# FFT layer and top-2 expert layer on one core: mixed last units, earlier re-reads, one addition on another engine

## The chip, the cores and the metric

One core of a Trainium2 chip runs the whole program. The metric is device time in microseconds (us): the median of three runs, lower is better. TensorE (PE) multiplies matrices, VectorE (DVE) and ScalarE (ACT) work on elements, GpSimd (POOL) works on elements and issues the indirect DMAs, SyncE (SP) issues the other DMAs.

## The reference

```python
X = np.fft.rfft(x, axis=1)                       # x: (8, 2496, 256)
y = np.fft.irfft(X * (filt_r + 1j * filt_i), n=2496, axis=1).astype(np.float32)
x = y.reshape(19968, 256)
logits = x @ w_gate + np.log1p(np.exp(x @ w_noise)) * noise      # 8 experts
top2 = the two largest logits of each row, softmaxed over the two
for e in range(8):
    for k in range(2):
        mask = top2[:, k] == e
        out[mask] += top2_w[mask, k, None] * (np.maximum(x[mask] @ w1[e], 0) @ w2[e])   # 256 -> 1024 -> 256
```

## The kernel before, in words

**The FFT side** takes the batches in turn, each as two halves `n` of 128 columns. A transform of 2496 points is a two-stage product, 39 by 64, written as matmuls. Between the forward and the inverse transform stands the filter: `kg1` (line 404) takes a product `p` from PSUM, multiplies it by `fr` and `fi`, and adds or subtracts the two results (lines 428 and 433). `kg2` (line 436) reads that result as weights of the matmuls of line 446. `kg1` and `kg2` run five times (`kg` 0 to 4) for each half `n`. For `n` under 4, the first two batches, the addition or subtraction is on GpSimd; afterwards it is on VectorE.

**The gate and the routing** turn the logits into lists of rows for each expert. The rows of `y` lie in DRAM. An expert unit gathers its rows from there with an indirect DMA of GpSimd (line 1156) into slots of one ring buffer (`slot("xg")`, four slots of 128 rows), and has them transposed by a DMA (line 1195).

**The expert side** runs in units of rows of one expert. `expert` (line 1332) does eight hidden blocks for a unit (PSUM tile `hps`, ScalarE's `hh` at line 1369, VectorE's `hl` at line 1370), then for each 128 rows 24 matmuls into `yps`, ScalarE's scaled copy (line 1396) and GpSimd's indirect scatter with addition to `out` (line 1397). All matmuls go as three of 16-bit halves (`_mm3`, lines 123 to 126). Scatters of one unit are declared independent of each other; a scatter of another unit waits until the last unit's have landed, since they may meet in a row of `out`.

**Sizes of units.** Early units have 512 rows, then come units of 1024, seven of 512, and at last the tail: units of 256 and 128 rows (`ENDS`, line 52). With these inputs 14 units of 256 and 4 of 128 are used. The other places for tail units, up to 17 and 8, are in a conditional part that isn't taken (line 1474). Each tail unit loads its own expert's weights from a scaled copy in DRAM (line 1270), into three places in turn.

**Scaling.** From the fifth batch on (`HALF`), rows and weights are scaled by powers of two and split into float16 halves. That wants the largest magnitude of each weight matrix (64 loads, line 595, with ScalarE's squares, line 599) and of the rows so far. Of the first two batches the rows' maxima are not taken when they are made: `load_y` (line 608) reads `y` back in 12 DMAs of 256-byte runs, and `top_y` (line 613) reduces each on VectorE into `ymax`. `powers` (line 553) turns a maximum into a power of two by a PE transpose, some ten small VectorE instructions and two small matmuls. It runs twice for the weights (`wmax`, into `wtab`) and once for each of the last four batches (`xscale`, line 579).

**What sets the order.** The preparation `wscales` (line 588) is a generator of steps. One step is taken for each four writes of the FFT side; the first gather of a unit of the fifth batch takes all that are left (line 1143). The program is written as one interleaved stream of FFT and expert work. The scheduler then orders each engine's queue by a simulated time, with priorities pinned for the first batches. Each engine runs its own queue strictly in order, SP's and POOL's DMA issues included.

Of the kernel before, what the change touches and what calls it, by code (L numbers as in the profile page):

```python
# [22 lines left out]
NB, S, D = 8, 2496, 256  # L23
# [26 lines left out]
NUNIT = (LEFT + E * (UNIT // 2 - 1)) // UNIT  # L50
USUAL = LEFT // UNIT
ENDS = (UNIT, USUAL, NUNIT), (UNIT // 2, E // 2, E)
SW = 32
YW = D + E
LR = 128
# [95 lines left out]
class Moe:  # L151
# [249 lines left out]
    def kg1(self, n, kg):  # L401
        nc, P, h = self.nc, self.P, n % 2
        th, tl = self.tt.pop((n, kg))
        Mh, Ml = self.cM
        p = self.ps("q3")
        if tl is None:
            nc.tensor.matmul(p, self.rM, th, start=True, stop=True)
        else:
            nc.tensor.matmul(p, Mh, th, start=True, stop=False)
            nc.tensor.matmul(p, Mh, tl, start=False, stop=False)  # L410
            nc.tensor.matmul(p, Ml, th, start=False, stop=True)
        if self.early:
            ab = P.tile([128, 2, 4, 128], F32, name="ab", tag="w2", bufs=4)
            a, b = ab[:, 0], ab[:, 1]
        else:
            a = P.tile([128, 4, 128], F32, name="a", bufs=2)
            b = P.tile([128, 4, 128], F32, name="b", bufs=1)
        p3 = p.rearrange("p (k d) -> p k d", k=4)
        fr = self.fr[:, h, 4 * kg:4 * kg + 4]
        fi = self.fi[:, h, 4 * kg:4 * kg + 4]  # L420
        if n >= 2:


            nc.scalar.copy(b[0:64], p3[64:128])
            nc.scalar.copy(b[64:128], p3[0:64])
            nc.vector.tensor_mul(a, p3, fr)
            nc.vector.tensor_mul(b, b, fi)
            (nc.gpsimd if n < 4 else nc.vector).tensor_sub(a, a, b)
        else:
            nc.vector.tensor_mul(a, p3, fr)  # L430
            nc.vector.tensor_mul(b[0:64], p3[64:128], fi[64:128])
            nc.vector.tensor_mul(b[64:128], p3[0:64], fi[0:64])
            (nc.gpsimd if n < 4 else nc.vector).tensor_add(a, a, b)
        self.zz[n, kg] = a

    def kg2(self, n, kg):
# [142 lines left out]
    def xscale(self, bt):  # L579

        nc = self.nc
        nc.vector.tensor_reduce(self.xm, self.ymax[:, :2 * bt + 2], axis=AX.XY, op=ALU.max)
        q = yield from self.powers(self.xm, 1, TX)
        t = self.xs[bt + 1] = self.cp.tile([128, 2], F32, name=f"xs{bt}")
        nc.vector.tensor_copy(t, q[:, :, 0])
        yield

    def wscales(self):


        nc, io, v = self.nc, self.io, self.nc.vector
# [39 lines left out]
        def pairs(first, then, n):  # L631
            old = []
            for i in range(n + 3):
                if i >= 3:
                    self.pin(then, *old.pop(0), hold=False)
                if i < n:
                    old.append((i, self.pin(first, i, hold=False)))
                yield

        yield from pairs(load, top, 8 * E)  # L640
        for a, t in enumerate((TW1, TW2)):
            q = yield from self.powers(self.wmax[:, a * E:a * E + E], E, t, True)
# [3 lines left out]
            else:  # L646
                v.tensor_mul(self.wtab[:, 2], self.wtab[:, 2], q[:, 1])
            yield
        yield from pairs(load_y, top_y, len(Y))
        self.scaled = True  # L650
        yield
        self.pin(load_all, 0)
# [483 lines left out]
    def gather(self, blk, i):  # L1136
# [12 lines left out]
        if self.tail(tabi):  # L1149
            w = self.wodd = (self.wodd + 1) % 3  # L1150
            if nt < BLK // 128:
                w = self.load_planes(tabi, s, w)
        xg = []
        for t in range(nt):
            x = self.slot("xg")
# [250 lines left out]
    def run(self):  # L1406
# [15 lines left out]
        def parts():  # L1422
# [20 lines left out]
            for s in range(SINGLE):  # L1443
                yield from cut(self.read_list(NB, s, BLK), NB)
            self.more = [self.nc.values_load(self.tabs[NB + 1 + i][0:1, 0, n:n + 1], min_val=0, max_val=E * CAPB * BLK // u)  # L1445
                         for i, (u, n, _) in enumerate(ENDS)]
            it = (self.read_list(NB + 1 + i, s, u) for i, (u, n, _) in enumerate(ENDS) for s in range(n))
            soon = [next(it)]
            while soon:
                soon += [b for b in (next(it, None),) if b]  # L1450
# [70 lines left out]
```

## Time and profile before

| | us |
|---|---|
| median of three runs | 2186.98 |
| the runs | 2180.4, 2186.98, 2194.4 |
| the profiled execution | 2191.23 |
| its span | 2189.4 |
| TensorE busy in the span | 2107.5 (96%) |
| VectorE, ScalarE, GpSimd busy | 1473.3, 1286.4, 1024.6 |

The span runs from the first to the last instruction of the profiled execution; 1.83 us of its time lie around the span. Busy times are sums over one engine. TensorE's idle time is what is left of the span when its busy time is taken off; a wait on another engine costs time only where TensorE, or the end of the program, waits for it.

### The profile page before, as it was taken

The page shows a single profiled execution, that of the slowest core. Times are in us where ns is not written, and L with a number is a line of the kernel's source. Part 1 is how long each engine was busy: PE and PEld are TensorE (multiplying, and loading weights), DVE is VectorE, ACT ScalarE, POOL GpSimd, SP SyncE. Part 2 cuts the span into 40 slices and gives each one's busy share as a digit, 9 for nine tenths or more (in the row PEclk, how much of TensorE's full clock was granted, in tenths as well). Part 3 has the DMA queues.
Part 4 walks back from the last instruction along what each step waited for, and adds up shares of the span by engine and source line. Part 5 has one row for each costly group of instructions (what it writes and reads, how often), then busy time and mean ns, then how long its engine had stood idle before and what let it go on. Part 6 is the DMA issues. An engine that isn't in the chain of part 4 may idle for free. (4 is left out here: it accounts for less than half of the span.)

```text
span 2189.4 us, 42880 instructions
## 1 busy us (share of the span) xinstructions
PE 2107.5 (96%) x14517; PEld 1596.5 (73%) x14517; DVE 1473.3 (67%) x3245; ACT 1286.4 (59%) x2505; POOL 1024.6 (47%) x946
## 2 busy tenths in 40 slices
PE   8779999999999999899999999999999999999996
PEld 6437888888888888666666666766666666667886
DVE  4866678767986787778766886579666664333443
ACT  6666774777567746665665556555566564333443
POOL 4133424533443343545544453544566555654653
PEclk9989999999999999999999999999999999999999
DMA  9688987999888866967766666856899999768996
GB/s 241 173 247 203 230 222 171 222 234 228 203 213 230 189 144 152 202 160 174 156 155 151 136 146 149 198 118 131 198 246 238 230 238 211 200 148 221 277 273 170
DMA packets 511675, 428.49 MB, mean 196 GB/s; under 512 B 215680, under 2 KB 397016, under 8 KB 511448
## 3 DMA queue, kind: packets, MB, share of 16 engines
q1 hardware_dynamic: 450135, 341.27, 59.2%
q0 software_dynamic: 61312, 84.40, 22.5%
q8 instruction: 116, 1.90, 0.4%
q14 instruction: 112, 0.91, 0.1%
HBM read 263.92 MB, written 122.03 MB: 176 GB/s over the span
## 5 line engine op out<-in xcount | busy, mean ns | idle before, releaser
L1397 POOL DMA_INDIRECT out<-stage,ids x316 | 527.3, 1669 | 339.8 <-ACT stage L1396 245.9
L1370 DVE SCALAR_TENSOR_TENSOR hl<-hps,hh 128x512 f16<-128x512 f32 (+3 forms) x712 | 432.2, 624 | 339.5 <-ACT hh L1369 279.1
L1156 POOL DMA_INDIRECT stage<-y,ids x316 | 348.4, 1103 | 538.2 <-DMA xt<-stage 425.5
L124 PE MATMUL yps<-w,hh 128*128 128x256 f16 (+1 forms) x2048 | 558.8, 279 | 9.0 <-ACT hh L1369 3.8
L125 PE MATMUL yps<-w,hh 128*128 128x256 f16 (+1 forms) x2048 | 553.2, 277 | 0.0
L126 PE MATMUL yps<-w,hl 128*128 128x256 f16 (+1 forms) x2048 | 543.4, 278 | 6.8 <-DVE hl L1370 6.5
L1369 ACT ACTIVATE hh<-hps 128x512 f16<-128x512 f32 (+3 forms) x712 | 375.6, 550 | 185.7 <-PE hps L126 161.6
L125 PE MATMUL hps<-mxl,w1h 128*128 128x512 f16 (+1 forms) x1024 | 394.3, 386 | 0.7 <-DVE mxl L1244 0.7
L126 PE MATMUL hps<-mxh,w1l 128*128 128x512 f16 (+1 forms) x1024 | 393.0, 385 | 0.0
L124 PE MATMUL hps<-mxh,w1h 128*128 128x512 f16 (+1 forms) x1024 | 385.5, 388 | 2.7 <-DVE hl L1370 1.7
L1396 ACT ACTIVATE stage<-yps,gt 128x256 f32<-128x256 f32 x316 | 143.2, 475 | 342.3 <-PE yps L126 169.8
L124 PEld LDWEIGHTS <-hh 128*128 128x128 f16 x1760 | 172.3, 98 | 51.3 <-ACT hh L1369 4.1
L126 PEld LDWEIGHTS <-hl 128*128 128x128 f16 x1760 | 171.5, 98 | 48.9 <-issue 3.0
L125 PEld LDWEIGHTS <-hh 128*128 128x128 f16 x1760 | 172.2, 98 | 38.1 <-issue 6.0
L126 PEld LDWEIGHTS yps<-w,hl 128*128 128x128 f32 x768 | 145.9, 192 | 15.8 <-DVE hl L1370 8.2
L124 PEld LDWEIGHTS yps<-w,hh 128*128 128x128 f32 x768 | 147.0, 192 | 12.5 <-ACT hh L1369 4.9
L125 PEld LDWEIGHTS yps<-w,hh 128*128 128x128 f32 x768 | 146.6, 192 | 4.4 <-issue 0.6
L542 ACT COPY yt<-q 117x1024 uint16<-117x1024 uint16 x96 | 90.8, 946 | 42.4 <-PE q L536 23.6
L126 PEld LDWEIGHTS <-w1l 128*128 128x128 f16 x640 | 62.6, 98 | 71.8 <-issue 1.1
L1226 DVE COPY stage<-xt 128x1024 uint16<-128x1024 uint16 (+2 forms) x174 | 109.8, 685 | 3.0 <-issue 1.9
L125 PEld LDWEIGHTS <-w1h 128*128 128x128 f16 x640 | 62.6, 98 | 54.0 <-issue 4.0
L124 PEld LDWEIGHTS <-w1h 128*128 128x128 f16 x640 | 62.6, 98 | 53.0 <-issue 6.2
(287 smaller groups left out, 4041.7 us busy)
## 6 DMA issues: line engine op xcount, KB each, us to landing
stage<-w SPq DMA_DIRECT2D x328, 256.0 KB
x<-x SPq DMA_DIRECT2D x88, 256.0 KB
fd<-c SPq DMA_DIRECT2D x77, 240.0 KB
fi<-wpl SPq DMA_DIRECT2D x18, 1024.0 KB
fx<-fd SPq DMA_DIRECT2D x140, 128.0 KB
out<-z SPq DMA_DIRECT2D x24, 702.0 KB
wp<-w SPq DMA_DIRECT2D x64, 256.0 KB
fr<-w SPq DMA_DIRECT2D x16, 1024.0 KB
```

The source lines that it names most:

```text
L124: nc.tensor.matmul(o, lh, rh, start=start, stop=False)
L125: nc.tensor.matmul(o, lh, rl, start=False, stop=False)
L126: nc.tensor.matmul(o, ll, rh, start=False, stop=stop)
L542: e = nc.scalar.copy(yt.bitcast(U16)[:, :k, :256].rearrange("p g (two d) -> p g two d", two=2), p.bitcast(U16)[:RP, :2 * m].rearrange("p ( ...
L1156: self.pin(lambda: nc.gpsimd.indirect_dma_start(out=x.bitcast(I32), out_offset=None, in_=self.y[:BLK + ready * ROWS], in_offset=bass.Indir ...
L1226: nc.vector.tensor_copy(xu.rearrange("p (t two) -> p two t", two=2), ent[3][0][:, 2 * kc:2 * kc + 2, :w])
L1369: hold(lambda: nc.scalar.activation(h, p, AF.Relu))
L1370: v = hold(lambda: nc.vector.scalar_tensor_tensor(l, p, 0.0, hf[0], op0=ALU.max, op1=ALU.subtract))
L1396: nc.scalar.activation(o, p, AF.Copy, scale=gate[:, t])
L1397: a = nc.gpsimd.indirect_dma_start(out=self.io["out"][:BLK + ready * ROWS], out_offset=bass.IndirectOffsetOnAxis(ap=ids[:, t:t + 1], axis= ...
```

## The change

Three parts. The tail units are taken from one list, `MIXED`, in which a unit of 256 rows with number s has key s and one of 128 rows has key 3s + 4, so that the 128-row units stand after the fifth, eighth, eleventh and fourteenth unit of 256; before they stood after all of them. A gather of 256 rows then skips a slot of the ring where a 128-row unit has left it at an odd place. The re-reads of `y` come ahead of the weights' maxima and the two weight chains in `wscales`. In batch 0 the addition of line 433 moves from GpSimd to VectorE; batch 1 stays on GpSimd. (Line numbers of the changed program are 1 higher from line 53 on, and 3 to 5 higher from line 582 on.)

```diff
--- before.py
+++ after.py
@@ -50,6 +50,7 @@
 NUNIT = (LEFT + E * (UNIT // 2 - 1)) // UNIT
 USUAL = LEFT // UNIT
 ENDS = (UNIT, USUAL, NUNIT), (UNIT // 2, E // 2, E)
+MIXED = sorted(((i, s) for i, (_, n, _) in enumerate(ENDS) for s in range(n)), key=lambda u: u[1] * 3 + 4 if u[0] else u[1])
 SW = 32
 YW = D + E
 LR = 128
@@ -425,12 +426,12 @@
             nc.scalar.copy(b[64:128], p3[0:64])
             nc.vector.tensor_mul(a, p3, fr)
             nc.vector.tensor_mul(b, b, fi)
-            (nc.gpsimd if n < 4 else nc.vector).tensor_sub(a, a, b)
+            (nc.gpsimd if 2 <= n < 4 else nc.vector).tensor_sub(a, a, b)
         else:
             nc.vector.tensor_mul(a, p3, fr)
             nc.vector.tensor_mul(b[0:64], p3[64:128], fi[64:128])
             nc.vector.tensor_mul(b[64:128], p3[0:64], fi[0:64])
-            (nc.gpsimd if n < 4 else nc.vector).tensor_add(a, a, b)
+            (nc.gpsimd if 2 <= n < 4 else nc.vector).tensor_add(a, a, b)
         self.zz[n, kg] = a
 
     def kg2(self, n, kg):
@@ -579,6 +580,7 @@
     def xscale(self, bt):
 
         nc = self.nc
+        assert self.seen
         nc.vector.tensor_reduce(self.xm, self.ymax[:, :2 * bt + 2], axis=AX.XY, op=ALU.max)
         q = yield from self.powers(self.xm, 1, TX)
         t = self.xs[bt + 1] = self.cp.tile([128, 2], F32, name=f"xs{bt}")
@@ -637,6 +639,8 @@
                     old.append((i, self.pin(first, i, hold=False)))
                 yield
 
+        yield from pairs(load_y, top_y, len(Y))
+        self.seen = True
         yield from pairs(load, top, 8 * E)
         for a, t in enumerate((TW1, TW2)):
             q = yield from self.powers(self.wmax[:, a * E:a * E + E], E, t, True)
@@ -646,7 +650,6 @@
             else:
                 v.tensor_mul(self.wtab[:, 2], self.wtab[:, 2], q[:, 1])
             yield
-        yield from pairs(load_y, top_y, len(Y))
         self.scaled = True
         yield
         self.pin(load_all, 0)
@@ -1150,6 +1153,8 @@
             w = self.wodd = (self.wodd + 1) % 3
             if nt < BLK // 128:
                 w = self.load_planes(tabi, s, w)
+        while (self.turns.get("xg", -1) + 1) % nt:
+            self.slot("xg")
         xg = []
         for t in range(nt):
             x = self.slot("xg")
@@ -1444,7 +1449,7 @@
                 yield from cut(self.read_list(NB, s, BLK), NB)
             self.more = [self.nc.values_load(self.tabs[NB + 1 + i][0:1, 0, n:n + 1], min_val=0, max_val=E * CAPB * BLK // u)
                          for i, (u, n, _) in enumerate(ENDS)]
-            it = (self.read_list(NB + 1 + i, s, u) for i, (u, n, _) in enumerate(ENDS) for s in range(n))
+            it = (self.read_list(NB + 1 + i, s, ENDS[i][0]) for i, s in MIXED)
             soon = [next(it)]
             while soon:
                 soon += [b for b in (next(it, None),) if b]
```

GpSimd's queue at the end of the used tail units, before. `out` is the scatter of line 1397, its `ids` name the unit, `x2` marks the two halves of a unit of 256 rows, and line 1156 is a gather.

```order
L1156 DMA stage_84<-y_60,ids_28778 128x264
L1397 DMA out<-stage_84,ids_28002 21104x256 x2
...
L1397 DMA out<-stage_84,ids_28198 21104x256
...
L1397 DMA out<-stage_84,ids_28392 21104x256
L1397 DMA out<-stage_84,ids_28584 21104x256
L1397 DMA out<-stage_84,ids_28778 21104x256
```

And now:

```order
L1161 DMA stage_84<-y_60,ids_28698 128x264
L1402 DMA out<-stage_84,ids_27946 21104x256
...
L1402 DMA out<-stage_84,ids_28142 21104x256 x2
...
L1402 DMA out<-stage_84,ids_28334 21104x256 x2
L1402 DMA out<-stage_84,ids_28528 21104x256 x2
L1402 DMA out<-stage_84,ids_28698 21104x256
```

The last four units were four single scatters; they are now three pairs and one single scatter.

VectorE's queue in batch 0, around the filter products of two steps, before (`q3` is PSUM, `fr` and `fi` the filter):

```order
L430 TENSOR_TENSOR ab_245<-q3_243,fr_80 128x512
L431 TENSOR_TENSOR ab_245<-q3_243,fi_81 64x512
L432 TENSOR_TENSOR ab_245<-q3_243,fi_81 64x512
L430 TENSOR_TENSOR ab_285<-q3_283,fr_80 128x512
L431 TENSOR_TENSOR ab_285<-q3_283,fi_81 64x512
```

And now:

```order
L431 TENSOR_TENSOR ab_245<-q3_243,fr_80 128x512
L432 TENSOR_TENSOR ab_245<-q3_243,fi_81 64x512
L433 TENSOR_TENSOR ab_245<-q3_243,fi_81 64x512
L434 TENSOR_TENSOR ab_245<-ab_245 128x512
L431 TENSOR_TENSOR ab_285<-q3_283,fr_80 128x512
```

Each step has a fourth instruction on VectorE ahead of the next step's first.

VectorE's queue at the first expert unit of the fifth batch, before (`xm<-ymax` begins the chain of the rows' scale, `pm`, `pe` and `pq` belong to it, `hl` is the expert block's low half):

```order
L582 TENSOR_REDUCE xm<-ymax 128x1
L615 TENSOR_REDUCE ymax<-wp 117x1 x2
L1202 SCALAR_TENSOR_TENSOR w1l<-stage,sc,w1h 128x512
L1370 SCALAR_TENSOR_TENSOR hl<-hps,hh 128x512
L398 TENSOR_TENSOR tl<-fx,th 128x512
L615 TENSOR_REDUCE ymax<-wp 117x1
```

And now, from the end of that chain (`xs`) on; the rows of `wtab` end a weight chain:

```order
L647 COPY wtab<-xm 128x8
L649 COPY wtab<-xm 128x8
L562 TENSOR_REDUCE pm<-xm 8x1
L563 TENSOR_SCALAR pm<-pm 8x1
L564 TENSOR_SCALAR pe<-pm 8x1
L566 TENSOR_SCALAR pe<-pe 8x1
L567 TENSOR_SCALAR pe<-pe 8x1
L568 TENSOR_SCALAR pq<-pe 8x1
L569 TENSOR_SCALAR pq<-pe 8x1
L570 TENSOR_SCALAR pq<-pq 8x2
L573 TENSOR_SCALAR pd<-ident,pq 8x8 x2
L647 COPY wtab<-xm 128x8
```

The re-reads have left this place, and both weight chains stand in it, the second with nothing between its instructions.

## Rows read from the trace of the kernel before

**Rows 1.** The page, part 1: busy us, share of the span and instructions of each engine.

```profile
PE 2107.5 (96%) x14517; PEld 1596.5 (73%) x14517; DVE 1473.3 (67%) x3245; ACT 1286.4 (59%) x2505; POOL 1024.6 (47%) x946
```

**Rows 2.** Windows late in the span; columns: window, length, engines' busy, clock, DMA, GB/s.

```profile
2150.00:2160.00 10.00, 9.44 (x117) 8.18 (x114) 4.37 (x17) 4.18 (x16) 4.93 (x6) 1.00 0.86 254
2160.00:2170.00 10.00, 9.35 (x124) 8.55 (x122) 5.38 (x22) 5.29 (x20) 2.21 (x4) 1.00 0.75 239
2170.00:2180.00 10.00, 4.04 (x52) 3.53 (x49) 1.50 (x6) 1.86 (x6) 3.09 (x2) 0.93 0.26 33
```

**Rows 3.** GpSimd's timeline at the end: start, us, instruction, [idle before <-releaser].

```profile
2155.76 1.56 POOL L1397 DMA_INDIRECT out<-stage,ids  x1 [0.30 <-ACT hh L1369]
...
2161.39 1.60 POOL L1397 DMA_INDIRECT out<-stage,ids  x1 [3.42 <-ACT hh L1369]
...
2169.94 1.59 POOL L1397 DMA_INDIRECT out<-stage,ids  x1 [6.30 <-ACT hh L1369]
2175.61 1.56 POOL L1397 DMA_INDIRECT out<-stage,ids  x1 [4.08 <-ACTq L1474]
2180.16 1.56 POOL L1397 DMA_INDIRECT out<-stage,ids  x1 [2.99 <-DMA out<-stage,ids]
```

**Rows 4.** The chain of waits that ended last: start us, us, what.

```profile
2175.61 3.80 DMA out<-stage,ids
...
2180.24 1.48 POOL out L1397
```

**Rows 5.** ScalarE's timeline: output copies of the last 256-row unit and the first and last 128-row ones.

```profile
2151.70 0.47 ACT L1396 ACTIVATE stage<-yps,gt 128x256 f32<-128x256 f32 x1 [1.41 <-PE yps L126]
...
2157.11 0.47 ACT L1396 ACTIVATE stage<-yps,gt 128x256 f32<-128x256 f32 x1 [0.75 <-issue]
...
2174.12 0.47 ACT L1396 ACTIVATE stage<-yps,gt 128x256 f32<-128x256 f32 x1 [0.86 <-PE yps L126]
```

**Rows 6.** Windows: forty microseconds around the first expert unit of the fifth batch.

```profile
870.00:910.00 40.00, 32.11 (x199) 23.47 (x198) 31.34 (x52) 22.20 (x41) 23.71 (x22) 0.96 1.08 209
```

**Rows 7.** Waits of TensorE, 870 to 900 us: line waited for, us, times, longest.

```profile
PE yps L126 <- DVE hl L1370: 4.2, 2, 3.4
```

**Rows 8.** VectorE's timeline there.

```profile
875.36 0.95 DVE L615 TENSOR_REDUCE ymax<-wp 117x1 f32<-117x768 bf16 x1 [1.86 <-DMA wp<-y]
...
888.75 1.22 DVE L615 TENSOR_REDUCE ymax<-wp 117x1 f32<-117x1024 bf16 x1 [1.48 <-DMA wp<-y]
```

**Rows 9.** Line 615: durations ns min/median/max, first and last start us, forms.

```profile
L615 DVE TENSOR_REDUCE ymax<-wp x12: 929/1204/1221, 839.2 to 890.0; 117x1 f32<-117x1024 bf16 x8, 117x1 f32<-117x768 bf16 x4
```

**Rows 10.** Tile xm, the power-of-two chains: columns as in rows 9.

```profile
L559 PE MATMUL xm<-ident,wmax x2: 270/272/273, 756.3 to 802.9; 128*8 128x128 f32 x2
L643 DVE COPY wtab<-xm x2: 159/163/167, 767.6 to 827.5; 128x8 f32<-128x8 f32 x2
```

**Rows 11.** Windows: where the re-reads go.

```profile
270.00:330.00 60.00, 58.20 (x371) 51.65 (x370) 45.03 (x85) 43.31 (x91) 18.95 (x19) 0.97 0.88 222
```

**Rows 12.** Costliest groups: xcount | busy us, mean ns | idle before.

```profile
L433 POOL TENSOR_TENSOR ab<-ab 128x512 f32<-128x512 f32 x10 | 12.7, 1271 | 9.5 <-DVE ab L432 9.5
...
L428 DVE TENSOR_TENSOR a<-a,b 128x512 f32<-128x512 f32 x60 | 41.1, 685 | 0.4
```

**Rows 13.** Waits of TensorE, 0 to 60 us.

```profile
PE q L446 <- POOL ab L433: 1.5, 1, 1.5
```

**Rows 14.** Windows of the first 100 us.

```profile
20.00:30.00 10.00, 7.54 (x35) 5.35 (x34) 7.21 (x12) 8.52 (x17) 9.71 (x9) 0.83 0.99 225
30.00:40.00 10.00, 9.39 (x68) 6.49 (x66) 9.20 (x15) 9.36 (x18) 7.24 (x7) 1.00 1.01 272
40.00:50.00 10.00, 10.00 (x47) 5.78 (x42) 4.31 (x7) 5.98 (x12) 3.37 (x3) 1.00 0.92 245
60.00:70.00 10.00, 6.87 (x27) 3.44 (x26) 6.06 (x16) 8.93 (x14) 0.38 (x1) 1.00 0.65 174
90.00:100.00 10.00, 6.95 (x40) 4.53 (x39) 9.93 (x33) 4.50 (x9) 3.58 (x3) 0.83 0.85 249
```

## The prediction

> **What bounds the kernel now.** I read the engines' shares first. TensorE is busy 2107.5 us of a span of 2189.4 [rows 1], so all idle time together is 81.9 us, and every gain must come out of that. The reader should see that a change which only reorders work cannot give more than a few of these microseconds, unless TensorE's clock changes. Then I read windows to find where the idle time lies. In the tail TensorE is nearly full until 2170 us (9.44 and 9.35 of 10), and then stops [rows 2]. So the tail is bound by TensorE to about 2174 us, and after that by something else. Third, the chain of waits and GpSimd's timeline say what: a chain of scatters [rows 3, 4]. In the middle, forty microseconds around the first unit of the fifth batch hold only 32.1 us of matmuls [rows 6]. In the first 100 us TensorE is between 6.9 and 10 of 10 busy [rows 14]. These are the three places that the change touches.
>
> **Part 1, the mixed tail.** A scatter of another unit waits for the landing of the one ahead. The last five scatters start at 2155.76, 2161.39, 2169.94, 2175.61 and 2180.16 [rows 3]: links of 5.63, 8.55, 5.67 and 4.55 us, 24.4 in all. The data come faster: from the last 256-row unit's second copy to the last 128-row unit's, ScalarE's copies start at 2151.70 and 2174.12 [rows 5], four units in 22.42 us, or 5.6 each. The scatter of the former's data, ready at 2151.70 + 0.47 = 2152.17, started at 2155.76 [rows 3], already 3.6 us behind, and the four links add 24.40 − 22.42 = 2.0. So the last scatter starts at 2180.16, while its data are ready at 2174.12 + 0.47 = 2174.59: 5.6 us late. From its start to the span's end are 9.2 us, which stay. The chain of waits says the same: the last step is the earlier scatter's flight, 3.80 us, and then the scatter [rows 4].
>
> In the new order the four last units are three pairs and a single. A pair of scatters counts as one link, since its two halves don't wait for each other, and it comes with 256 rows of matmuls instead of 128. Since 512 rows took 22.42 us, 256 take by estimate half of that, so the time per link grows from 5.6 to some 11 us. That is longer than the longest link seen, 8.55. Only the last, single scatter is close: its data come some 5.6 us after the pair's second copy, against links between 4.55 and 8.55. With one of the three shorter links it waits 0 to 0.1 us; with 8.55 it waits 3. I take 0.5, since the long link falls where weights are still being loaded (the windows 2150 to 2170 move 254 and 239 GB/s, the last one 33 [rows 2]). So the wait falls from 5.6 to 0.5: 5.1 us gained, 2.6 at worst. The hand-overs between small units (TensorE loses 0.56 and 0.65 us in the two windows of rows 2) are spread among larger units; I take 0.4 us of gain, between 0 and 1. **Part 1: −5.5 us, between −2.5 and −6.5.**
>
> The flight itself can be weighed against the Trainium skill. The row says 3.80 us from a scatter's start to the next step [rows 4]. By "DMA: Bandwidth & Descriptors", section "Anatomy of one DMA — SWDGE (gpsimd) path", a DMA costs some 2.0 us and its bytes at 436 GB/s, an estimate of 2.3 us for 128 KB. With that a link would be the scatter's 1.6 us and 2.3 more, 3.9 us, shorter than the units' pace; no wait could build up in the old order, part 1 would give the 0.4 of the hand-overs alone, and the sum would be −3. The measured links, 4.55 to 8.55 us, contradict it [rows 3].
>
> **Part 2, the re-reads first.** It takes 12 DMAs and 12 reductions of 1.2 us, some 14 us of VectorE, out of 839 to 890 us [rows 9], and puts them behind the first batches' routing: in VectorE's queue they now stand next to instructions that ran at 200 to 330 us. What they cost now: the forty microseconds lose 40 − 32.1 = 7.9 us of TensorE [rows 6]. VectorE stands still there for the re-reads' DMAs, 1.86 and 1.48 us [rows 8], and the expert blocks' `hl` wait behind it in the queue; TensorE waits 4.2 us for `hl` [rows 7]. I count all 7.9 as gone. Against it: the two weight chains, which lay apart and took 767.6 − 756.3 = 11.3 and 827.5 − 802.9 = 24.6 us among other work [rows 10], are now taken at this place, behind the rows' chain. Fourteen small instructions of a chain at 0.16 to 0.27 us (the ends of the range shown for `L643` and `L559` [rows 10]) are 2.2 to 3.8 us if nothing lies between them. The second chain has nothing between, and the copies of the scale on GpSimd and the weight splits of the first unit wait for it: +3 us, from +1 (hidden behind other matmuls) to +8 (all three chains in a row are exposed). And the re-reads' DMAs can stop VectorE in their new place as well. There TensorE has 1.8 us idle in 60 and VectorE is 75% busy [rows 11], so it has less room than at 870. I take half of the 4.2 us of `hl` waits, +2, from 0 to +4. **Part 2: −7.9 + 3 + 2 = −3 us, between −6 and +4.**
>
> **Part 3, the addition on VectorE.** GpSimd gives up 10 additions of 1.271 us; VectorE gets 10, and the same operation on the same shape takes it 0.685 us elsewhere [rows 12], so 6.9 us. Where is room? Between 20 and 50 us VectorE is busy 7.21 + 9.20 + 4.31 = 20.7 of 30 us [rows 14]: the 6.9 fit as a sum, but not in 30 to 40, where 0.8 is free. There the steps come later, each addition by up to 0.7 us less the 0.6 by which it is shorter and the time it no longer stands behind other GpSimd work. TensorE waited once, 1.5 us, for a GpSimd addition [rows 13], and this wait goes or gets shorter. I take the middle of −1.5 and +2.5: **part 3: +0.5 us.** Its bounds are −1 and +3; beyond them lies a rival.
>
> **Other moves.** The number of instructions of every other kind is unchanged, but the scheduler orders the whole stream anew, on each engine. I cost that at nothing, with ±4 us: half of the 7.9 us that one such neighbourhood was seen to lose.
>
> **The sum.** −5.5 − 3 + 0.5 = −8 us against the profiled execution's 2191.2, which gives 2183.2. That execution lies 4.25 us above the median of 2186.98, so the forecast for a median is 2179.
>
> **The rivals.**
> - **The last scatter is held by something that the order doesn't remove.** The new last scatter still follows another unit's, and a long link (8.55) is as possible as a short one. For it: one link of four was long. Against it: the long one overlaps the loads of weights. Then part 1 gives 2.5 and, with the middle at zero, the sum is about −2: 2185.
> - **The weight chains and the new places eat the gain.** The chains cost +8, the re-reads +4, the order +2, against −7.9 and the tail's −5.5: about 0 to +1, 2188. For it: all three chains now lie ahead of the first scaled unit, and GpSimd's gathers and scale copies queue behind that. Against it: FFT matmuls can be taken meanwhile.
> - **Slower: VectorE becomes the bound of batch 0.** In 30 to 40 us it is 92% busy [rows 14]; if every addition goes to the path, its 6.9 us are paid, less the 1.5 us wait. Then TensorE stands still a little in each step, and the clock may fall with it. At nearly the same busy share, 6.87 and 6.95, one window shows the full clock and another 0.83 [rows 14]. The latter is the mean of the two levels with a third of the time at the lower, 1.2 GHz; a full window at that share loses about 1.7 us. Three more such windows make +5, and with 6.9 − 1.5 that is +10, against −8.5 for the other parts; where part 2 gives nothing either, it stands against −5.5 alone, +4.5: 2191.5, slower than before. It decides from the point where a step on VectorE takes longer than on TensorE. By the Trainium skill, "TensorE: Matmul & The Clock Gate", section "Part 1: The HAM clock gate", the throttled clock is the default and activity releases it; the row at 0.83 agrees that gaps can bring it back.
>
> **How the numbers follow.** Chances: the forecast 0.55 (2172 to 2184); the held scatter 0.15 (2185); the eaten gain 0.18 (2188); VectorE's bound 0.09 (2191.5); something not seen, either way, 0.03. The range is 2166 to 2195. Its lower end takes all parts at their best (−6.5 − 6 − 1 = −13.5, so 2173.5) and the order's −4, with 3.5 for the median's own scatter; its upper end is the slow rival with the same 3.5 added. One per cent is about what a measurement of this kernel can tell from no change: below 2165 or above 2209. All named cases lie within it: faster 0.06, same 0.90, slower 0.04.
>
> **What would show it.** Right: the last scatter starts within 1 us of the end of its data's copy, and 9.2 us follow; the windows 870 to 910 hold over 36 us of matmuls; the additions take 0.68 us on VectorE and the step's pace in batch 0 stays. Wrong: the last scatter waits for a landing; TensorE waits at the first unit of the fifth batch for `w1l`, `xs` or the scale copies; more windows below 150 us at 0.83.

## The result, and the profile after

The changed kernel takes **2216.35 us** (median; 2214.89 to 2223.29), the kernel before on the same chip 2189.4 (2180.4 to 2194.4): a ratio of 1.0134, with a 95% interval from 1.0093 to 1.0175. By the ratio it is slower by some 29 us (20 to 38). 2179 was forecast, 8 us faster, and the result lies above the whole range. The profiled execution has a span of 2215.8 us, 26.4 longer than before.

Part 1 of the page after, to set beside [rows 1]:

```profile
PE 2118.8 (96%) x14517; PEld 1601.3 (72%) x14517; DVE 1482.6 (67%) x3255; ACT 1286.6 (58%) x2505; POOL 999.6 (45%) x936
```

The same 14517 matmuls take 11.3 us more of busy time, and idle time grows from 81.9 to 97.0. VectorE has 10 instructions more, GpSimd 10 fewer: part 3 is there. For the place of the loss, windows of stretches, first of the kernel before, then after (window, length, busy of PE, PEld, DVE, ACT, POOL, clock, DMA share, GB/s):

```profile
410.00:750.00 340.00, 332.25 (x2142) 290.48 (x2142) 256.52 (x531) 247.25 (x509) 137.87 (x112) 0.99 0.90 220
870.00:950.00 80.00, 72.11 (x461) 51.53 (x459) 62.47 (x103) 53.83 (x95) 35.52 (x34) 0.98 0.91 194
```

```profile
410.00:750.00 340.00, 322.92 (x2021) 280.89 (x2021) 253.04 (x525) 238.73 (x494) 130.63 (x108) 0.98 0.89 216
870.00:950.00 80.00, 71.48 (x427) 53.48 (x426) 49.23 (x107) 49.61 (x96) 34.19 (x37) 0.94 0.74 182
```

The reader should see two things. Between 410 and 750 us, where the prediction placed nothing, TensorE loses 332.25 − 322.92 = 9.3 us and a little clock. At 870 to 950, where 7.9 us were to be won, it wins nothing. Windows of 10 us, summed up (idle time, and busy time times the missing share of the clock), give where the 26.4 us lie: up to 410 us +0.4 (3.6 more idle, 3.2 less lost to the clock); 410 to 750 us +9.3 idle and +3.5 clock; 750 to 960 us +1.2 and +2.7; from there to 2110 us +2.2. Some 7 are left for the tail. The count of matmuls done agrees: TensorE is some 19 us behind the kernel before at 2120 us and some 26 at 2160.

**410 to 750 us.** ScalarE's waits for the loads of the weights' maxima, before and after (engine, line waited for, us, times, longest):

```profile
ACT wp L599 <- DMA wp<-w: 26.0, 16, 3.4
```

```profile
ACT wp L601 <- DMA wp<-w: 38.6, 22, 5.1
```

The squares stood at 187.4 to 734.8 us before. Line 601 is their place after; the rows under it are of ScalarE's timeline:

```profile
L601 ACT ACTIVATE wp<-wp x64: 617/633/677, 299.3 to 887.4; 128x512 f32<-128x512 f32 x64
```

```profile
501.44 0.63 ACT L601 ACTIVATE wp<-wp 128x512 f32<-128x512 f32 x1 [3.39 <-DMA wp<-w]
...
530.18 0.63 ACT L601 ACTIVATE wp<-wp 128x512 f32<-128x512 f32 x1 [2.73 <-DMA wp<-w]
...
542.67 0.63 ACT L601 ACTIVATE wp<-wp 128x512 f32<-128x512 f32 x1 [5.14 <-DMA wp<-w]
```

A square takes 0.63 us, but ScalarE stands up to 5.14 us ahead of one, and what is behind it in the queue (`hh` of the expert blocks, copies of the FFT) stands too. TensorE waits for that work. In this stretch its waits for ScalarE sum to 5.9 us before and 14.5 after; the difference, 8.6, is nearly all of the 9.3 us lost. One such wait, behind the square that follows the one at 501.44:

```profile
504.27 0.63 ACT L601 ACTIVATE wp<-wp 128x512 f32<-128x512 f32 x1 [2.10 <-DMA wp<-w]
...
504.89 0.56 ACT L448 COPY G<-q 128x512 f32<-128x512 f32 x1
```

```profile
505.51 0.50 PE L344 MATMUL q<-xh,hl 117*120 117x512 f32 x1 [2.59 <-ACT G L448]
```

The re-reads are earlier (186.9 to 278.0 us, against [rows 9]), so all 64 squares are later. The stretch holds no more of them than before, 44 against 43; it is the waits for their loads that grew.

**870 to 950 us.** The stretch of [rows 6], the one behind it, and TensorE's steps of the chains after:

```profile
870.00:910.00 40.00, 33.70 (x216) 30.08 (x218) 20.29 (x59) 19.67 (x43) 18.46 (x19) 0.95 0.75 175
890.00:930.00 40.00, 32.11 (x184) 22.50 (x183) 21.74 (x54) 19.91 (x38) 20.86 (x25) 0.87 0.73 167
```

```profile
L577 PE MATMUL xm<-pd,small x12: 245/251/374, 894.7 to 912.7; 8*128 8x8 f32 x8, 1*128 1x1 f32 x4
L560 PE MATMUL xm<-ident,wmax x2: 273/273/273, 895.2 to 907.0; 128*8 128x128 f32 x2
```

The hole of [rows 6], 32.11 of 40, is there again, 20 us later: 890 to 930 held 36.65 before. The two weight chains, apart at 756 and 803 us in [rows 10], now stand in a row from 895.2 to 912.7, and the granted clock falls to 0.87. TensorE's longest waits here are 3.5 us for a copy of ScalarE and 1.6 us for a chain's `pd`, so the chains are a part of what fills the hole and not shown to be all of it.

**The tail.** Windows after, and GpSimd's timeline:

```profile
2120.00:2130.00 10.00, 8.36 (x79) 6.71 (x77) 4.55 (x14) 4.08 (x12) 4.87 (x6) 1.00 0.98 278
...
2140.00:2150.00 10.00, 9.28 (x86) 8.15 (x84) 3.67 (x11) 3.97 (x11) 6.55 (x8) 1.00 0.88 272
2150.00:2160.00 10.00, 8.51 (x89) 7.64 (x88) 3.85 (x12) 3.70 (x11) 6.15 (x8) 1.00 1.06 279
2160.00:2170.00 10.00, 7.19 (x76) 6.04 (x74) 3.91 (x12) 3.73 (x12) 6.09 (x7) 0.95 1.03 250
```

```profile
2130.68 0.19 POOL L1109 CAST ids<-lt 128x1 int32<-128x1 f32 x1 [5.03 <-DMA lt<-lst]
...
2139.99 0.64 POOL L1109 CAST ids<-lt 128x2 int32<-128x2 f32 x1 [4.57 <-DMA lt<-lst]
...
2173.60 0.64 POOL L1109 CAST ids<-lt 128x1 int32<-128x1 f32 x1 [4.96 <-DMA lt<-lst]
...
2202.19 1.57 POOL L1402 DMA_INDIRECT out<-stage,ids  x1 [0.67 <-ACT stage L1401]
2207.04 1.56 POOL L1402 DMA_INDIRECT out<-stage,ids  x1 [3.28 <-ACT stage L1401]
```

```profile
2205.78 0.47 ACT L1401 ACTIVATE stage<-yps,gt 128x256 f32<-128x256 f32 x1 [0.86 <-PE yps L127]
```

The last scatter starts 2207.04 − 2206.25 = 0.8 us behind its data, not 5.6 as in [rows 3, 5]. What the mixed order was expected to win at the end of this queue, it wins. But these data are ready 31.7 us later than before (2206.25 against 2174.59), and the whole is 26.4 us longer. GpSimd, which turns a unit's list of rows into addresses before it can gather them, stands for the list (`lt`) time and again, and TensorE, full until 2150 us before, has holes from 2120 on.

### The profile page after: what moved, and what is told of

Its sections match the earlier page's. It is cut to its first block, busy times and chain, and to the rows that moved or that the text cites. A ratio compares the mean times of both kernels' runs of the same rounds, so it can differ in the third digit from the quotient of the medians.

```text
span 2215.8 us, 42844 instructions
## 1 busy us (share of the span) xinstructions
PE 2118.8 (96%) x14517; PEld 1601.3 (72%) x14517; DVE 1482.6 (67%) x3255; ACT 1286.6 (58%) x2505; POOL 999.6 (45%) x936
## 4 chain that ended last, share of the span: by engine, by line
PE 80%; DMA 7%; DVE 5%; ACT 4%; issue 3%; SPq 1%; POOL 1%; another core or an unknown queue 0%; ACTq 0%; DVEq 0%; POOLq 0%
PE hps L127 11%; PE hps L125 11%; PE yps L125 11%; PE yps L127 11%; PE hps L126 11%; PE yps L126 11%; DMA wp<-w 3%; PE q L447 2%; PE q L511 1%; DMA stage<-w 1%; DVE hl L1375 1%; PE u L458 1%; PE q L336 1%; DMA wp<-y 1%; PE q L535 1%
## 5 line engine op out<-in xcount | busy, mean ns | idle before, releaser
L1402 POOL DMA_INDIRECT out<-stage,ids x316 | 521.9, 1652 | 355.2 <-ACT stage L1401 266.9
```

The source lines that it names most:

```text
L1402: a = nc.gpsimd.indirect_dma_start(out=self.io["out"][:BLK + ready * ROWS], out_offset=bass.IndirectOffsetOnAxis(ap=ids[:, t:t + 1], axis= ...
```

## The experiments

Ratios are to the kernel before on the same chip, with 95% intervals. "PE" and "ACT waits" in what follows are TensorE's busy time and ScalarE's waits for `wp<-w` in 410 to 750 us, from the views above.

### One part at a time

e1 has the `MIXED` order (with the skipped slots) alone, e2 the moved line alone, e3 the addition alone, e4 the last two together.

> Only the mixed order of the tail units, the other two parts left as before. Theory A (the tail's mixture itself costs: in the trace of the change the tail runs from +18 to +26 us behind the kernel before): 6 to 10 us slower than before, 2195 to 2200 us, with TensorE gaps of 1.5 to 3 us around each 128-row unit that stands between 256-row ones. Rival (the tail's loss comes from the state in which the middle leaves the kernel, or from the new order of the whole stream): 4 to 6 us faster than before, as forecast for this part.

> Only the re-reads of y ahead of the weights' maxima. Theory B (the weights' loads and squares, moved from 187-735 us to 299-887 us, now stop ScalarE's queue where TensorE waits for it): 14 to 19 us slower than before, about 2203 to 2208 us, ScalarE's waits for wp<-w near 67 us instead of 46. Rival (the addition on VectorE and the schedule that follows from it is what costs in the middle): within 5 us of before.

> Only batch 0's filter addition on VectorE. Theory B: the same as before within 3 us, since in the trace of the change the first 450 us run 1 to 5 us ahead of the kernel before. Rival (VectorE as the bound of batch 0, or a reordered middle): 10 us slower or more.

> The change without its mixed tail. If the parts add up: the time of the re-reads alone, 14 to 19 us slower than before, and 8 to 11 us faster than the whole change. If the tail's loss is not the mixture's, the same as the whole change, about 2216 us.

| | median us | ratio | PE | ACT waits |
|---|---|---|---|---|
| e1 mixed tail | 2195.09 | 1.0019 [1.0005, 1.0033] | 331.79 | 29.6 |
| e2 re-reads first | 2212.01 | 1.0097 [1.0070, 1.0123] | 321.00 | 42.2 |
| e3 addition on VectorE | 2188.71 | 0.9986 [0.9970, 1.0003] | 329.77 | 35.0 |
| e4 e2 and e3 | 2213.53 | 1.0099 [1.0075, 1.0122] | 319.82 | 45.5 |

By these ratios the moved line is most of the loss: +21 us by itself. The mixed tail costs 4, the addition gains up to 7 or costs up to 1.

### How the re-reads' place costs

Three edits ask how: one empty step more ahead of the weights (e5, other ring places), a longer lead of the loads over the squares (e6), the old order but with the re-reads ahead of the chains (e7).

```diff
 e5          yield from pairs(load_y, top_y, len(Y))
+            yield
 e6  pairs: for i in range(n + 4): if i >= 4: ... (3 before)
 e7          yield from pairs(load, top, 8 * E)
+            yield from pairs(load_y, top_y, len(Y))
             for a, t in enumerate((TW1, TW2)):   # the chains
```

> The re-reads first, and one empty step between them and the weights, so that each weight load and square stands 16 steps later than before instead of 15: the two buffer tags take turns as before, and every fourth square falls on the same place. Theory B1 (the odd shift: loads and squares now take the other buffer tag than the transform's tiles next to them): most of the 21 us comes back, to within 6 us of before. Theory B2 (the squares, in order on ScalarE, wait for loads that land 3 to 9 us after issue, and stand among work that TensorE waits for, at whatever step): no more than 6 us comes back, 2204 us or more.

> The re-reads first, and each load issued four steps ahead of its square or reduction instead of three. Theory B2: ScalarE's waits for wp<-w fall from 60-70 us to under 35, and the time by 8 to 15 us, to about 2197 to 2204. Theory B1: unchanged within 5 us (2207 to 2217). Either way more buffers of the two tags are held, which can cost the transform some us.

> The weights' loads and squares where they were before (from step 0 on), then the re-reads of y, then the two weight chains; the assertion in xscale left out. Theory B in any form (the shift of the weights' squares costs): 2186 to 2196, most of the 21 us back. Rival (what costs is that the two weight chains now come last, at the first unit of the fifth batch): no more than 6 us back, 2204 or more, with the loss at 860 to 920 us.

e5: 2217.06, 1.0136 [1.0092, 1.0179]; e6: 2214.75, 1.0116 [1.0077, 1.0156]: neither ring places nor a longer lead mend it (PE 322.08 and 321.15, ACT waits 48.5 and 45.3). e7: 2197.29, 1.0028 [1.0007, 1.0048]:

```profile
410.00:750.00 340.00, 331.94 (x2127) 290.24 (x2125) 255.58 (x521) 246.06 (x505) 133.56 (x111) 0.99 0.88 218
870.00:950.00 80.00, 68.89 (x417) 48.00 (x417) 55.73 (x113) 48.71 (x89) 36.56 (x37) 0.87 0.71 165
```

With the weights in their old place the middle is as before. What is left of the loss is at 870 to 950, where e7 too has all three chains in a row: 68.89 against 72.11, at 0.87 of the clock against 0.98. Here TensorE does wait for the chains, 9.4 us for `pd`.

### Without the squares

e9 is e2, e10 the kernel before, both without the 64 loads and squares; e17 is e2 with the loads and without the squares; in e18 VectorE takes the maxima of the loads.

```diff
-            nc.scalar.activation(t, t, AF.Square, accum_out=self.wquart[:, i % 4:i % 4 + 1])
+        v.memset(self.wquart, 0.25)                        # e9, e10, e17: once
+            v.tensor_reduce(self.wquart[:, i % 4:i % 4 + 1], t, axis=AX.X, op=ALU.max, ...)   # e18
```

> The re-reads first, and the 64 weight loads and squares left out (the squares' sums are set to a constant, so the weights' scales are not the true ones; the steps, the reductions of the sums and the chains stay). Theory B3 (the squares, wherever they stand among expert work, cost TensorE 0.5 to 1 us each through ScalarE's queue; the re-reads first push 15 more of them into that stretch): the 15 us of the stretch from 490 to 860 us disappear and more with them, about 2175 to 2185, and within 8 us of the kernel before without squares. Rival (the new order as such costs, through the schedule): 15 us or more behind the kernel before without squares.

> The kernel before with the 64 weight loads and squares left out in the same way. Theory B3: 8 to 20 us faster than before, 2170 to 2182, since ScalarE waited 46 us for these loads. Rival: the same as before within 5 us, since before the squares stood where they cost nothing.

> The re-reads first; the 64 weight loads for the maxima stay, ScalarE's 64 squares of them are left out (the quarter maxima are a constant). If the squares in ScalarE's queue, each waiting for its load with expert work queued behind it, are what costs: as without both, 2186 to 2194 us, and TensorE's idle time between 410 and 750 us is 4 to 7 us, not 17 to 23. If the loads' own traffic (16 MB, and their places in SyncE's queue) costs: 2203 to 2214 us with idle time of 14 us or more.

> The re-reads first, and the maxima of the 64 weight loads taken by VectorE (a reduction by magnitude each, and two tiny instructions for every fourth; the scale is then from 5 times the largest magnitude, not from the sum of squares), so that no weight load is waited for in ScalarE's queue. If ScalarE's in-order queue is the mediator: idle time of TensorE between 410 and 750 us falls from 17 to 23 to at most 10 us, and the time is 2188 to 2200 us. If any engine that waits for these loads hurts as much, since the expert blocks' hl on VectorE then stand behind the load: 2205 to 2220 us.

| | median us | ratio | PE |
|---|---|---|---|
| e9 | 2190.21 | 0.9987 [0.9964, 1.0010] | 336.23 |
| e10 | 2171.53 | 0.9915 [0.9882, 0.9948] | 336.49 |
| e17 | 2191.44 | 1.0043 [1.0023, 1.0064] | 333.39 |
| e18 | 2224.65 | 1.0204 [1.0183, 1.0225] | 317.21 |

(The kernel before ran at 2180.66 beside e17 and e18, at 2190.9 beside e9 and e10: the chips differ, the ratios tell.) The rows of e17 and of e18, and VectorE's wait in e18:

```profile
410.00:750.00 340.00, 333.39 (x2157) 291.93 (x2156) 258.43 (x529) 223.34 (x428) 134.89 (x112) 0.99 0.92 224
```

```profile
410.00:750.00 340.00, 317.21 (x1969) 273.12 (x1968) 263.28 (x563) 204.42 (x387) 133.96 (x106) 0.97 0.83 206
```

```profile
DVE wquart L600 <- DMA wp<-w: 36.2, 16, 5.5
```

At 410 to 750 us the loss goes where the squares are gone. e17 keeps e2's order and all the loads, and TensorE holds 333.39, not 321.00. TensorE's own waits say on whom it stands: in e2 15.5 us for ScalarE and 2.9 for VectorE, in e17 2.0 and 4.5, in e18 5.5 and 17.0. In e18 the wait for the loads went with the maxima, from 42.2 us on ScalarE to 36.2 on VectorE, in front of the `hl` of the expert blocks, and TensorE's waits went with it. So the loss comes through the queue of the engine that stands for the loads. (e18 also gives VectorE some 13 us more work in the stretch: it is busy 263.28 us against 250.54 in e2.)

The loads by themselves are not free. They take turns in the buffers of the transform's `th` and `tl`, so that in e17, where nobody reads them, ScalarE and VectorE still stand for them before they can write there:

```profile
ACT th L520 <- DMA wp<-w: 14.8, 5, 4.8
ACT th L397 <- DMA wp<-w: 6.1, 4, 1.9
DVE tl L521 <- DMA wp<-w: 5.7, 3, 4.3
```

With no loads at all e9 holds 336.23, which is 2.8 us more. By the ratios e17 is still 9 us slower than the kernel before and 12 slower than e9 (on another chip). And e18, forecast at 2205 to 2220 by the theory that any engine which waits hurts as much, is 44 us slower: at 870 to 950 it holds 63.92 at 0.79 of the clock.

In the whole time the answer is not so clean. I had put that without squares the two orders agree; e9 and e10 still differ by 18.7 us. That theory fell in its total and holds for 410 to 750 us alone. By the windows, e9 has lost 8 us against e10 by 410 us, nearly all of it at 180 to 290 us, where its re-reads stand (100.96 against 105.28 of 110, at 0.95 of the clock against 0.98). But e2 and e17 have the same re-reads there, also without a square beside them, and hold 104.84 and 105.66: the re-reads' place alone does not cost these 8 us, and what does stays open. e9 loses 5.2 more at 870 to 950 (74.62 against 79.78).

That last number bears on the prediction's largest term. In e10 the re-reads still come last, at 815.0 to 864.4 us, and VectorE waits 6.2 us for them; yet TensorE has only 1.4 us idle in 840 to 910, against 7.9 in the kernel before. First e10, then the kernel before:

```profile
840.00:910.00 70.00, 68.62 (x444) 54.76 (x443) 54.64 (x89) 44.97 (x83) 35.26 (x32) 1.00 0.84 189
```

```profile
840.00:910.00 70.00, 62.11 (x388) 49.99 (x387) 52.44 (x100) 40.30 (x77) 31.29 (x31) 0.98 0.89 183
```

Re-reads that come last do not by themselves make the hole of [rows 6].

### Is it the place of the squares?

e13 is the kernel before with 15 empty steps ahead of the weights, which moves the squares as far without an early re-read. e15 is e2 with the first 30 weight loads two to a step, so that the later ones come at their old steps.

```diff
+        for _ in range(len(Y) + 3):                        # e13
+            yield
         yield from pairs(load, top, 8 * E)
-                yield                                      # e15, in pairs
+                if i >= fast or i % 2:
+                    yield
```

> The kernel before with 15 empty steps ahead of the weights' maxima, as many as the re-reads of y take: the weights' loads and squares, the chains and the re-reads all come 15 steps later, in the old order, and no re-read is early. Theory P (place): the squares cost TensorE 12 to 18 us between 490 and 860 us because they stand 110 us later, whatever stands ahead of them; then the matmuls run 12 to 18 us behind the kernel before by 865 us, and the time is 2205 to 2222 us, since chains and re-reads also stand at the first unit of the fifth batch. Rival R (re-reads): the early re-reads themselves disturb what follows; then the matmuls keep within 4 us of the kernel before until 865 us, only the unit at 880 to 920 us costs 5 to 13, and the time is 2193 to 2203 us.

> The re-reads first alone, but the first 30 of the weights' loads come two to a step, so that from some 450 us on the weights' steps stand where they stand in the kernel before, and the chains too. Theory P (place): no loss between 490 and 860 us, and the chains stand apart again, so the forty microseconds at 870 to 910 give their gain: 2182 to 2193 us. Rival R (re-reads): the early re-reads cost 12 to 18 us wherever the weights stand: 2200 to 2212 us. Between the two if the double pace from 300 to 450 us costs something by itself: 2194 to 2200 us.

e13: 2201.75, 1.0038 [1.0015, 1.0062]; e15: 2211.91, 1.0074 [1.0047, 1.0101]. Windows and ScalarE's wait of e13, then of e15:

```profile
410.00:750.00 340.00, 325.35 (x2076) 283.23 (x2075) 255.63 (x519) 245.66 (x513) 125.81 (x104) 0.99 0.90 217
```

```profile
ACT wp L599 <- DMA wp<-w: 41.7, 22, 5.1
```

```profile
410.00:750.00 340.00, 317.15 (x1991) 275.32 (x1989) 244.25 (x514) 236.50 (x497) 128.19 (x108) 0.98 0.90 217
```

```profile
ACT wp L600 <- DMA wp<-w: 42.4, 19, 6.3
```

By their times both fall to the re-reads' side (2193 to 2203 and 2200 to 2212 were expected of it), and e15 by its stretch too: with the later weight loads back at their old steps the waits stay at 42.4 us and the loss at 332.25 − 317.15 = 15.1. So the place of the squares is not the whole cause. But e13, in which nothing is early, has waits of 41.7 us and loses 6.9 us there, more than the 4 that were allowed. Place and early re-reads each disturb the stretch.

The two also test the chains. e15's stand apart again, at 786.6 and 833.3 us, and 870 to 910 hold 38.43; but 910 to 950 hold only 33.25, since TensorE waits 6.8 us for the rows' own scale `xs`. e13's stand at the first unit, at 873.6 and 890.2 us, and 870 to 950 hold 73.99, more than before. So chains in a row are not needed for the hole, and in e13 they add nothing to it; what sets it stays open.

Of the kernels with the squares on ScalarE seven have waits of 26.0 to 35.0 us and PE at 329.5 to 332.3 (before, e1, e3, e7 and, below, e8, e11, e12), and eight waits of 38.6 to 48.5 us and PE at 317.2 to 325.4 (the change, e2, e4, e5, e6, e13, e14, e15). One stands apart, e16, with 33.2 us and 318.79: the waits for these loads are the largest thing that goes with the loss, but not all of it. Within the eight the loss does not follow them (48.5 us of waits with 322.08, 42.4 with 317.15).

**What stays open:** why an order with early re-reads brings the loads late to ScalarE. The scheduler's order of TensorE's own queue is another one there: by 530 us the kernel before has done 1243 matmuls of the FFT side with gate and routing, e7 and e13 1253, but e2 1196, e15 1177 and e9 1205, at some 1660 to 1700 of the expert side in all six. FFT work comes later where re-reads are early. In e9 that costs nothing in this stretch, so it does not explain the loss alone, and no experiment held this order fixed.

### The tail's lists

e8 is e1 with the lists of rows read two units ahead; e12 the same without the mixed order; e11 is e8 with the addition on VectorE; e14 the whole change with lists two ahead; e16 is e14 with e15's pace.

```diff
-        ids = self.P.tile([128, n, nt], I32, name="ids", bufs=6)
+        ids = self.P.tile([128, n, nt], I32, name="ids", bufs=7)
-            soon = [next(it)]
+            soon = [next(it), next(it)]
```

> The mixed tail alone (first experiment), with the tail units' row lists read two units ahead instead of one. In the trace of the change a list's tiny DMA lands 8 to 9 us after issue, behind the 2 MB of weights in SP's queue, and a 128-row unit gives only half the time to cover list, gather and transposes. If that is why the mixture costs: 4 to 8 us less than the mixed tail alone, 2187 to 2191. If not: the same, 2193 to 2198.

> The kernel before, unmixed, with the tail's lists read two units ahead. If the list is late for 128-row units among 256-row ones only: the same as before within 3 us. If it is late everywhere in the tail: 4 to 8 us faster, as the mixed tail with lists two ahead, and the mixture itself then gains nothing.

> The mixed tail with lists two units ahead, and batch 0's addition on VectorE; the re-reads of y stay last, as before. If the parts add up (0.9987 and 0.9986): 4 to 8 us faster than before, 2182 to 2186. If their new schedules interfere: the same as before within 4 us.

> The whole change, with the lists of the tail units read two units ahead, not one. Theory: the tail's loss of the change (5 to 8 us against the re-reads-first kernel) is late lists, and goes: 2204 to 2210 us, with tail windows 2120 to 2160 at 9.5 or more. Rival: in the whole change the tail's gaps have another cause (the place of the weights' loads in the queue): 2212 to 2220 us.

> The whole change with both mends: the weights' loads two to a step until they have caught up, and the lists two units ahead. By theory P and the late lists: 2178 to 2188 us, the kernel before less what the re-reads first and the mixed tail give. By rival R: 2198 to 2208 us.

| | median us | ratio | PE 2120 to 2140 | GpSimd's waits for lists |
|---|---|---|---|---|
| e1 mixed | 2195.09 | 1.0019 [1.0005, 1.0033] | 17.44 | 31.9 |
| e8 mixed, lists two ahead | 2187.03 | 0.9987 [0.9962, 1.0012] | 19.78 | 14.8 |
| e12 lists two ahead alone | 2188.80 | 0.9998 [0.9979, 1.0018] | 20.00 | 16.0 |
| e11 e8 and the addition | 2186.42 | 0.9982 [0.9963, 1.0001] | 19.79 | 16.0 |
| e14 change, lists two ahead | 2216.81 | 1.0094 [1.0061, 1.0126] | 19.78 | 20.6 |
| e16 e14 with e15's pace | 2216.98 | 1.0093 [1.0061, 1.0126] | 19.78 | 25.6 |

(The waits are those of line `ids` for `lt`, 2050 to 2180 us; the kernel before had 28.1 beside a full PE, 20.00, the change 41.9 and 18.36. PE is of 20 us.) Windows of e1, then of e8, and GpSimd's waits in the two:

```profile
2120.00:2140.00 20.00, 17.44 (x175) 15.68 (x174) 6.78 (x20) 7.82 (x22) 12.48 (x16) 1.00 0.95 263
```

```profile
2120.00:2140.00 20.00, 19.78 (x203) 17.52 (x201) 9.46 (x29) 9.17 (x27) 10.83 (x13) 1.00 1.15 288
```

```profile
POOL ids L1107 <- DMA lt<-lst: 31.9, 7, 7.7
```

```profile
POOL ids L1107 <- DMA lt<-lst: 14.8, 6, 4.6
```

Late lists make the holes of the mixed tail. Read one unit further ahead they give TensorE 19.78 − 17.44 = 2.3 us back in these 20 alone. e8 is 0.3% quicker than e1 by the ratios, but their intervals overlap and they ran on different chips, so in the whole time this is likely and not shown. Without the mix the same reading ahead takes the waits from 28.1 to 16.0 us and gains nothing (e12): between the larger units these waits were hidden. In the whole change the holes at 2120 to 2160 close as well (19.78 and 19.95 of 20), but e14's time lies above its 2204 to 2210, since its TensorE was 23 us behind by 718 us already (by the count of matmuls done), the change itself 14. By the ratios e14 is as slow as e4: what is left is the re-reads' loss. e16 shows the same; its theory, 2178 to 2188, fell with e15's.

e11 is the best of all. It beats the change by some 30 us, and the kernel before by 4 us at the median, with an interval that just reaches 1: not shown faster than before.

## Why the prediction was wrong, point by point

- **What bounds the kernel: right.** TensorE, with 82 us of idle time as all that could be won. That a new order can lose more than it can win stood neither in my first paragraph nor in my range.
- **The scatters of part 1: right in the change, not always.** 0.5 us of waiting was forecast for the last scatter, 0.8 measured (0.8 in e8, 0.7 in e11). In e1 it was 5.2 and in e14 3.2: there the last scatter waited for the landing of the one ahead, as the first rival had it. **The term was wrong in sign**: −5.5 forecast, +4 in e1, some 7 in the change's tail. I priced the end of GpSimd's queue and not its head. A unit of 128 rows gives half the matmuls to hide the next unit's list, addresses, gather and weights. At the end of the program nothing larger followed it; in the middle a unit of 256 rows does. e8 shows it for the lists. The step that failed is "the hand-overs between small units are spread among larger units; I take 0.4 us of gain".
- **Part 2 is the step that failed most.** −3 us, between −6 and +4, was forecast (by its own terms the lower end is −7.9 + 1 = −6.9); e2 measured +21 [+15, +27]. Its three terms:
  - "I count all 7.9 as gone": they moved. After the change 890 to 930 us hold the 32.11 that 870 to 910 held before. I had put the hole down to the re-reads because VectorE waits for them there; in e10 they also come last, and there is no hole.
  - The chains, +3 (to +8): right as a risk. e7 has the chains' place without the squares' shift, costs 6, and waits 9.4 us for them. In the change TensorE waits 1.6 us for them; in e13 they stand at the same unit and add nothing, and in e15 the hole is there without them. So they are not shown to be what filled it again. The clock there was 0.94 against 0.98 over 80 us.
  - "Half of the 4.2 us of `hl` waits, +2": the wrong place. VectorE waited 9.2 us for the early re-reads, as feared, but up to 410 us TensorE lost 0.4. The price is paid at 410 to 750 us, 12.8 us, where the prediction has no term: that is the term it put at nothing. I moved 12 DMAs and 12 reductions forward and did not ask what they displace: 64 loads and 64 squares, 110 us later, each of which stops ScalarE's queue if its load has not landed. ScalarE waited 16 times in this stretch before and 22 times after, 26.0 and 38.6 us in all, and TensorE's waits for ScalarE rose by 8.6 us. e17 and e18 show that the loss comes through the queue of the engine that takes the maxima; why the loads come later in the new order stays open.
- **Part 3: right in size.** The additions take 0.69 us on VectorE (0.68 forecast), and the first 100 us go at the same pace (TensorE is some 1.5 us ahead at 100 us by the count of matmuls done):

```profile
L434 DVE TENSOR_TENSOR ab<-ab x10: 691/692/1368, 21.8 to 49.1; 128x512 f32<-128x512 f32 x10
```

```profile
20.00:30.00 10.00, 8.12 (x46) 5.42 (x45) 9.68 (x15) 9.80 (x19) 7.52 (x7) 1.00 1.05 261
30.00:40.00 10.00, 8.16 (x55) 5.28 (x56) 9.64 (x16) 8.11 (x15) 0.00 (x0) 1.00 1.00 295
```

  VectorE is fuller than in [rows 14] (9.68 and 9.64 of 10), yet the first window kept the full clock, where it had 0.83 before. e3 lies between −7 and +1 us, which holds the +0.5 forecast, near its end. VectorE did not become the bound.
- **Other moves, "at nothing, ±4": far too narrow.** A new order of the whole stream cost TensorE 7 to 15 us at 410 to 750 us in every order with early re-reads or late weights that kept the maxima.
- **The rivals.** None had this size. "The weight chains and the new places eat the gain" named a mechanism that e7 shows, at 2188. The slow rival, VectorE's bound, did not come. The sign I wrote down as a way to be wrong, TensorE waiting at the first unit of the fifth batch, was seen, but it is the smaller part.

## What to carry to other kernels

A step moved to the front of an in-order sequence moves everything behind it: price the steps that it displaces, above all those on which an engine stands for a load, before the step itself. When small pieces are mixed among large ones, ask what must arrive per piece (lists, gathers, weights) and whether half the work hides it; reading one piece further ahead closed the holes here. When a wait stands beside a hole, test whether the hole goes with it before its whole length is counted as a gain. And a kernel whose main engine is 96% busy can lose far more by a new order than it can win, so the range has to be wide on that side.

## What the runs showed of the hardware

- A list of 1 KB took nine microseconds to be of use. In the tail after, SyncE issues a unit's weights and then the next list:

```profile
2140.49 1.15 SPq L1275 DMA_DIRECT2D fr<-wpl  x2
2142.20 0.01 SPq L1103 DMA_DIRECT2D lt<-lst  x1
```

  GpSimd, which had stood for that list for 3.41 us, went on at 2151.33: some 9.1 us after the issue, behind the 2 MB of weights in the same queue (two matrices of 256 by 1024 with 4 bytes for each element). How long the same list takes with nothing ahead of it was not measured.
- Standing for loads was no cheaper on VectorE than on ScalarE, with expert blocks that use both: 42.2 us of waits on ScalarE (e2) and 36.2 on VectorE (e18) went with 11 and 15 us less of TensorE than in the kernel before.
- Loads without a reader still held engines up through their buffers: 20.9 us on ScalarE and 6.9 on VectorE at 410 to 750 us of e17, while TensorE was busy 333.39 of 340 us, against 336.23 with no loads (e9).
